# A new written order for the first batch of a fused attention and gated-layer kernel

## The chip, the cores and the metric

The kernel runs on one core of a Trainium2 chip. TensorE multiplies matrices into PSUM, VectorE and ScalarE do element-wise work, and SyncE's queue issues nearly all transfers between the chip's main memory and SBUF. All numbers are 32-bit floats. The metric is the device time of one execution in microseconds (us), and a kernel's time is the median of its runs. The profile is of one execution; its clock starts with the first instruction (the span).

## The reference

For 8 batches of 8 heads, x (512 tokens by 64) and a state (32 rows by 64) look at each other; both results stand under each other, 544 rows a batch, and the heads side by side, 512 columns. A two-layer network with a gate follows.

```python
scores = scale * x @ state.T            # 512 x 32 for each head
xread  = softmax(scores) @ state
scores2 = scale * state @ x.T           # 32 x 512
sread  = softmax(scores2) @ x
y = concat(xread, sread)                # 544 rows a batch, heads side by side: 4352 x 512 (8 batches)
h = y @ w_in                            # d_ff = 2048
g = h * erf(softplus(h))
out = g @ w_out                         # back to 512
```

The kernel doesn't form xread. It multiplies the state of a batch with w_in first ("mixing": m = state times a slice of w_in, for each head) and gets h as the attention weights times m.

## The kernel before, in words

The hidden width 2048 is cut into 4 groups of 512, each group into 4 blocks of 128. Batches 1 to 7 run in a loop of two groups at a time, with seven products in place of eight (L275, L383, L489, L641 and their helpers). Batch 0 is different: no weight is in SBUF yet, so its steps follow the loading of the weights, and nearly everything is interleaved by hand. Its steps are small functions with names, and one string, order0 (L1053 to L1074), lists the names; each is run in that order, and each engine then executes its share in the order written (in_order, L1083). A wait therefore holds up all that stands behind it on the same engine. An engine's own share, not the list as a whole, decides: two neighbours on different engines run side by side.

The names: x0 to x3 turn the tokens (TensorE), st turns the state; s0, s1 are scores, tm0, tm1 turn them, max, less, exp, sum, inv, norm make the softmax over states, ta0, ta1 turn the weights back. An ending _a or _v says whether ScalarE (L756) or VectorE (L757) copies a result from PSUM. m00, m01, m02, m10, m12 and so on mix (group, first block; L908), x and y are halves. h01 is hidden block 1 of group 0 (L919), soft01 its Softplus (L952), erf01 its Erf (L954; erf00+ does two blocks at once, L957), mul01 the product of both (L959, VectorE). p021 is the second-layer product of token block 2, hidden block 1, group 0 (L926): 16 for each group, each of two passes. big, wt (Exp, L854), wz (an inverse), wn, tw and read are the attention in the other direction, u0 and u1 turn the states of the other batches.

i0 to i7 and o0 to o7 are pieces of w_in and w_out, each needing two ScalarE steps (a0 at L166 and a1 at L168) and three VectorE steps (v0 to v2, L171 to L173); i0+ is the second half of piece i0. A `get` issues the load of the next piece (L156) into one of three buffers, in a fixed order of pieces; it waits until the buffer is read. lxq10 to lxq17, lxq2 and lx1 load x of batches 1 and 2 in two layouts, xq1v turns one on VectorE (2.30 us). q, qm, qe, qs, qr, n0, n1, cm and ca are the attention, mixings and sums of batch 1. kept stores w_in in main memory, from where the loop reloads it.

A name with a number, as `4*to1`, first issues so many "warm" products of the identity by itself (warm, L192, through lead) into the bank that the step will use. They compute nothing that is used; each is two passes of 128 columns.

The functions on ScalarE need a table: Exp, Softplus and Erf each have one of their own, and changing from one to another puts an ACT_TABLE_LOAD into the program. So the order of ScalarE's steps decides how many loads there are.

The last 40 names of the list are put in order together with the loop's first instructions. After the list come the first hidden products of batch 1 (L489, with copies at L495 and L504), between them the rest of group 3's p steps, and then the read of batch 1 (L275).

Of the kernel before, what the change touches and what calls it, by code (L numbers as in the profile page):

```python
# [17 lines left out]
def kernel(  # L18
# [78 lines left out]
    def load_xq(b, hs=range(H)):  # L97
# [11 lines left out]
    st = const.tile([P, B, P], F32, name="st")  # L109
    away0 = ring[:, 1, 0].rearrange("p k i t -> p (k i t)")  # L110
    st0 = away0[:, 512:640].rearrange("p (g d) -> p g d", g=2)
    x0 = xin.tile([P, NC, H, D], F32, name="x").rearrange("p c h d -> p (c h d)").rearrange(
        "p (h c d) -> p h c d", h=H, c=NC)
# [931 lines left out]
    for _ in range(3):  # L1045
# [5 lines left out]
    ready = next0()  # L1051

    order0 = """  # L1053
        first x0 x2 x2_v x0_a x3 x3_v st x1 i0a0 st_v s1 i0v0 i0a1 i0v1 x1_a s10_v i0v2 s11_a 2*s0
        tm1 i0+a0 i0+a1 i0+v0 i0+v1 s00_a max1 s01_a tm0 less1 exp1 m00y m001_a i0+v2 max0 i1a0 sum1
        4*to1 m01x m010_a less0 exp0 o0a1 m00x 4*to1 m01y m011_a inv1 norm1 i1a1 4*ta1 u0 o0a0 sum0
        inv0 m000_v norm0 ta0 get ta1_v h001 ta0_a lxq13 o1a1 h01 i1v0 i1v1 soft01 i1v2 lxq16 m02
        m020_a m021_v o0v0 h000 o0v1 soft00 u1 u1_v h02 erf00+ h03 o0v2 mul01 big1 p001 mul00 u0_v
        p011 big0 p010 p030 o1a0 big soft03 lxq17 o1v0 p000 soft02 erf02+ p031 p020 p021 o1v1 o1v2
        wt0 mul03 wt1 p023 wz mul02 wn0 get i2a0 i2v0 get i2a1 i2v1 i3a1 get lxq14 lxq10 p033 p032  # L1060
        tw0 p013 tw0_a p002 i3a0 i2v2 m10 m101_a p022 o2a0 m100_v h10 o2a1 h11 i3v0 i3v1 i3v2 m12
        o2v0 p012 o2v1 m121_v lxq11 get p003 lxq15 lxq12 soft10 m120_v h13 wn1 soft11 o3a0 erf10+
        h12 o3a1 o2v2 mul11 mul10 p110 p100 soft13 p111 p120 get p101 o3v0 o3v1 p131 soft12 o3v2
        erf12+ mul13 p123 p103 i4a0 i4v0 i4a1 mul12 p132 p133 i4v1 i4v2 get i5a1 i5a0 i5v0 i5v1 get
        o4a0 p113 m20 p130 p121 m201_v m200_v h20 i5v2 m22 m220_v m221_v o4a1 o4v0 o4v1 get get p102
        soft20 o5a1 o4v2 p112 o5a0 o5v0 tw1 tw1_v o5v1 erf20 mul20 h21 h23 i6a0 h22 p220 soft21 p210
        o5v2 soft23 erf23 mul23 p230 soft22 erf22 xq1v get i7a1 read read_v p203 mul22 p223 i6a1
        i6v0 i6v1 i6v2 i7a0 p213 p202 q erf21 q1_a qm7 get p222 q0_a p232 qm1 mul21 o6a1 n1 o6a0
        p212 n11_v p231 i7v0 i7v1 n10_a m30 cm0 m300_a m301_a qm0 qm6 p211 p221 get qm8 qe2 qm3 qm5
        qe1 p200 p201 qe3 qm2 qm4 i7v2 n0 n00_a h30 qe0 qs1 qs0 qs2 h31 n01_a m32 p122 soft30 m321_a  # L1070
        m320_a get p233 o6v0 o6v1 o6v2 soft31 erf31 h32 mul31 h33 p311 cm1 qr0 o7a0 qr2 get erf30
        mul30 p331 p301 qr1 cm3 ca0 qr3 p310 soft32 erf32 o7a1 mul32 get ca1 ca2 o7v0 o7v1 lx1 p330
        ca3 p321 soft33 p300 kept erf33 o7v2 lxq2 mul33 cm2 p320
    """  # L1074
    steps0 = order0.split()
    for n, name in enumerate(steps0):
# [246 lines left out]
```

## Time and profile before

| what | value |
|---|---|
| time, median of 3 runs (lowest, highest) | 720.24 us (720.0, 721.69) |
| the profiled execution's own time | 720.67 us |
| its span, first to last instruction | 718.9 us |
| TensorE busy | 710.0 us (99%) |
| VectorE busy | 541.7 us (75%) |
| ScalarE busy | 378.8 us (53%) |
| moved by the transfers | 74.64 MB |
| first second-layer product (L926) | 29.30 us |
| first copy at L495, after the list | 111.95 us |
| read of batch 1 (L275) | 129.99 us |

The profile counts TensorE as busy from a product's start to its modelled end, so short waits between products hide in a busy time of 99%. They show when the starts of rows are set against the number of passes between them. A row names the engine, the source line, the operation, out<-in tiles, the sizes and the count; what stands in brackets is idle time of the engine before it, and what ended it.

### The profile page before, as it was taken

Reading aid. Unit: us, or ns where it says so; the run is one execution under the profiler, and the core shown is the slowest. Engines: PE = TensorE matmul, PEld = TensorE weight load, DVE = VectorE, ACT = ScalarE, POOL = GpSimd, SP = SyncE. Lnnn points to the kernel's source line nnn. Section 1 sums busy time; section 2 is a strip of 40 time slices with the busy share of each in tenths; the row PEclk is TensorE's granted clock in tenths of the full one; section 3 lists DMA queues with packets and bytes.
Section 4 is the critical chain, followed back from the end, with each engine's and each line's share of the span. In section 5 each row is a group of like instructions: output and inputs, shape, how many; then the busy total and the mean of one; then the engine's idle time right before and its main releaser. Section 6 shows DMA issues by size and latency. Waiting matters only on the chain.

```text
span 718.9 us, 10934 instructions
## 1 busy us (share of the span) xinstructions
PE 710.0 (99%) x4275; PEld 560.5 (78%) x4275; DVE 541.7 (75%) x878; ACT 378.8 (53%) x537; POOL 25.2 (4%) x34
## 2 busy tenths in 40 slices
PE   8899999999999999999999999999999999999998
PEld 6344346688878878887888878887888888889997
DVE  5887799889868987788776967697877757664533
ACT  5898986746464625545446436462464535442340
POOL 0000000000100000000000000000000000000000
PEclk9999999999999999999999999999999999999999
DMA  8695597660349163513623280614242321102100
GB/s 268 193 247 200 170 321 178 149 179 30 45 88 220 25 130 51 148 45 89 101 30 146 60 144 5 176 27 131 50 103 84 86 52 26 34 30 30 22 10 29
DMA packets 144067, 74.64 MB, mean 104 GB/s; under 512 B 123024, under 2 KB 132624, under 8 KB 142480
## 3 DMA queue, kind: packets, MB, share of 16 engines
q1 hardware_dynamic: 139152, 65.89, 33.3%
q0 software_dynamic: 4032, 7.34, 7.5%
q8 instruction: 33, 0.54, 0.3%
q10 hardware_dynamic: 832, 0.72, 0.3%
q14 instruction: 18, 0.15, 0.1%
HBM read 49.81 MB, written 20.45 MB: 98 GB/s over the span
## 4 chain that ended last, share of the span: by engine, by line
PE 87%; ACT 7%; DMA 3%; DVE 2%; issue 1%; SPq 0%; ACTq 0%
PE o L641 47%; PE h L489 13%; PE at L489 10%; PE h L534 3%; PE o L616 3%; PE o L926 3%; DMA raw<-in_moe_w_out_dram 2%; PE h L383 2%; PE at L383 2%; ACT L952 1%; PE at L275 1%; ACT raw L168 1%; ACT ring L952 1%; ACT L954 1%; PE h L919 1%
## 5 line engine op out<-in xcount | busy, mean ns | idle before, releaser
L641 PE MATMUL o<-w_out,ring 128*128 128x256 f32 x896 | 203.0, 379 | 0.0
L641 PEld LDWEIGHTS o<-w_out,ring 128*128 128x128 f32 x896 | 169.8, 190 | 24.9 <-DVE ring L1126 0.8
L641 PE MATMUL o<-raw,ring 128*128 128x256 f32 x672 | 161.4, 381 | 0.0
L641 PEld LDWEIGHTS o<-raw,ring 128*128 128x128 f32 x672 | 126.5, 190 | 25.9 <-ACT m L385 9.2
L482 ACT ACTIVATE ring<-ring 128x512 f32<-128x512 f32 x112 | 70.6, 631 | 59.7 <-DVE ring L472 59.1
L489 PE MATMUL h<-aT,m 128*128 128x256 f32 x336 | 81.9, 379 | 0.3 <-ACT ring L495 0.3
L1126 DVE TENSOR_TENSOR ring<-ring 128x1024 f32<-128x1024 f32 (+1 forms) x61 | 70.7, 1201 | 4.5 <-ACT ring L546 4.5
L489 PEld LDWEIGHTS h<-aT,m 128*128 128x128 f32 x336 | 63.8, 190 | 10.6 <-issue 1.2
L472 DVE TENSOR_TENSOR ring<-ring,at 128x512 f32<-128x512 f32 x84 | 57.1, 680 | 16.9 <-PE at L489 15.2
L926 PE MATMUL o<-w_out,ring 128*128 128x512 f32 x128 | 59.9, 602 | 0.1
L626 DVE TENSOR_TENSOR ot<-uv,o 128x256 f32<-128x256 f32 (+1 forms) x56 | 30.9, 552 | 30.1 <-PE o L641 28.1
L472 DVE TENSOR_TENSOR ring<-ring,h 128x512 f32<-128x512 f32 x56 | 38.0, 678 | 20.0 <-PE h L489 19.9
L664 ACT COPY ot<-o 128x256 f32<-128x256 f32 x28 | 10.4, 373 | 77.9 <-PE o L641 77.9
L704 POOL DMA_DIRECT2D out_dram<-ot x28 | 24.5, 946 | 654.9 <-DVE ot L626 556.1
L926 PEld LDWEIGHTS o<-w_out,ring 128*128 128x128 f32 x128 | 23.2, 189 | 28.1 <-issue 22.4
L626 DVE TENSOR_TENSOR ot<-ot,o 128x256 f32<-128x256 f32 x56 | 22.2, 416 | 27.9 <-ACT ot L664 27.7
L504 ACT COPY ring<-h 128x512 f32<-128x512 f32 x28 | 16.4, 587 | 47.9 <-PE h L489 47.9
L673 DVE TENSOR_TENSOR ring<-ring 128x512 f32<-128x512 f32 x56 | 38.6, 689 | 1.4
L674 DVE TENSOR_TENSOR ring<-ring 128x512 f32<-128x512 f32 x56 | 36.2, 684 | 0.0
L385 ACT COPY m<-h 128x512 f32<-128x512 f32 x13 | 7.6, 586 | 46.3 <-PE h L383 46.1
L546 ACT ACTIVATE ring<-ring 128x2048 f32<-128x2048 f32 x16 | 30.5, 1904 | 0.0
L489 PE MATMUL h<-sy,sx 128*128 128x256 f32 x112 | 28.7, 379 | 0.0
(201 smaller groups left out, 963.7 us busy)
## 6 DMA issues: line engine op xcount, KB each, us to landing
w_in<-kept_in SPq DMA_DIRECT2D x7, 2048.0 KB, 8.3
out_dram<-ot SPq DMA_DIRECT2D x33, 256.0 KB, 2.2
raw<-in_moe_w_in_dram SPq DMA_DIRECT2D x16, 512.0 KB, 5.3
raw<-in_moe_w_out_dram SPq DMA_DIRECT2D x8, 1024.0 KB, 5.1
xq<-in_x_dram SPq DMA_DIRECT2D x112, 64.0 KB, 3.2
x<-in_x_dram SPq DMA_DIRECT2D x56, 128.0 KB, 3.1
out_dram<-ot POOLq DMA_DIRECT2D x28, 256.0 KB, 4.5
sc<-xT SPq DMA_DIRECT2D x112, 32.0 KB, 1.9
```

Source lines behind the costliest of these rows:

```text
L383: nc.tensor.matmul(out=ps[k][e][q, :], lhsT=st[r, b, q], rhs=of_group[g][r, :, i, :], start=True, stop=True)
L472: add = lambda o, x, y: nc.vector.tensor_tensor(o, x, y, op=ALU.add)
L482: nc.scalar.activation(out=s[k], in_=hs[k], func=ACTF.Softplus)
L489: nc.tensor.matmul(out=out[:, i], lhsT=x[:, q:q + P], rhs=y, start=(first and i == 0), stop=(i == 1), skip_group_check=not first)
L546: nc.scalar.activation(out=s, in_=s, func=ACTF.Erf)
L626: add = lambda o, x, y: tt(o, x, y, op=ALU.add)
L641: nc.tensor.matmul(out=out, lhsT=lhs[:, i, :], rhs=rhs[:, g, i, :], start=(start and i == 0), stop=(i == GF - 1), skip_group_check=not start)
L673: return [lambda: tt(S1, A21, A22, op=ALU.add), lambda: tt(S2, S1, A11, op=ALU.subtract), lambda: tt(S3, A11, A21, op=ALU.subtract), lambd ...
L674: lambda: tt(S3, A11, A21, op=ALU.subtract), lambda: tt(S4, A12, S2, op=ALU.subtract)]
L704: nc.gpsimd.dma_start(out=rows[2 * h + r][:, c], in_=ot[:, c], accum_op=ALU.add)
L926: nc.tensor.matmul(out=acc[r], lhsT=gT[g][:, i, P * r:P * r + P], rhs=w_out[:, GF * g + i, :], start=(made_of[r] == 1), stop=(made_of[r] = ...
L1126: nc.vector.tensor_tensor(s[:, ks], s[:, ks], hs[:, ks], op=ALU.mult)
```

## The change

The string order0 is written anew, and nothing else. The steps are the same but for some copies that change their engine, and for the warm products: besides the eight of the first step, 14 before (two ahead of s0, four ahead of m01x, m01y and ta1 each), 13 after (three ahead of tm1, six ahead of m01x, four ahead of ta0). The tokens' turns, the two score halves, the pieces' conversions, the p steps, the loads of x of batch 1 (lxq, lx1), the load of xq for batch 2 and kept all change places. The order of the pieces' loads itself stays.

```diff
@@ -1051,26 +1051,26 @@
     ready = next0()
 
     order0 = """
-        first x0 x2 x2_v x0_a x3 x3_v st x1 i0a0 st_v s1 i0v0 i0a1 i0v1 x1_a s10_v i0v2 s11_a 2*s0
-        tm1 i0+a0 i0+a1 i0+v0 i0+v1 s00_a max1 s01_a tm0 less1 exp1 m00y m001_a i0+v2 max0 i1a0 sum1
-        4*to1 m01x m010_a less0 exp0 o0a1 m00x 4*to1 m01y m011_a inv1 norm1 i1a1 4*ta1 u0 o0a0 sum0
-        inv0 m000_v norm0 ta0 get ta1_v h001 ta0_a lxq13 o1a1 h01 i1v0 i1v1 soft01 i1v2 lxq16 m02
-        m020_a m021_v o0v0 h000 o0v1 soft00 u1 u1_v h02 erf00+ h03 o0v2 mul01 big1 p001 mul00 u0_v
-        p011 big0 p010 p030 o1a0 big soft03 lxq17 o1v0 p000 soft02 erf02+ p031 p020 p021 o1v1 o1v2
-        wt0 mul03 wt1 p023 wz mul02 wn0 get i2a0 i2v0 get i2a1 i2v1 i3a1 get lxq14 lxq10 p033 p032
-        tw0 p013 tw0_a p002 i3a0 i2v2 m10 m101_a p022 o2a0 m100_v h10 o2a1 h11 i3v0 i3v1 i3v2 m12
-        o2v0 p012 o2v1 m121_v lxq11 get p003 lxq15 lxq12 soft10 m120_v h13 wn1 soft11 o3a0 erf10+
-        h12 o3a1 o2v2 mul11 mul10 p110 p100 soft13 p111 p120 get p101 o3v0 o3v1 p131 soft12 o3v2
-        erf12+ mul13 p123 p103 i4a0 i4v0 i4a1 mul12 p132 p133 i4v1 i4v2 get i5a1 i5a0 i5v0 i5v1 get
-        o4a0 p113 m20 p130 p121 m201_v m200_v h20 i5v2 m22 m220_v m221_v o4a1 o4v0 o4v1 get get p102
-        soft20 o5a1 o4v2 p112 o5a0 o5v0 tw1 tw1_v o5v1 erf20 mul20 h21 h23 i6a0 h22 p220 soft21 p210
-        o5v2 soft23 erf23 mul23 p230 soft22 erf22 xq1v get i7a1 read read_v p203 mul22 p223 i6a1
-        i6v0 i6v1 i6v2 i7a0 p213 p202 q erf21 q1_a qm7 get p222 q0_a p232 qm1 mul21 o6a1 n1 o6a0
-        p212 n11_v p231 i7v0 i7v1 n10_a m30 cm0 m300_a m301_a qm0 qm6 p211 p221 get qm8 qe2 qm3 qm5
-        qe1 p200 p201 qe3 qm2 qm4 i7v2 n0 n00_a h30 qe0 qs1 qs0 qs2 h31 n01_a m32 p122 soft30 m321_a
-        m320_a get p233 o6v0 o6v1 o6v2 soft31 erf31 h32 mul31 h33 p311 cm1 qr0 o7a0 qr2 get erf30
-        mul30 p331 p301 qr1 cm3 ca0 qr3 p310 soft32 erf32 o7a1 mul32 get ca1 ca2 o7v0 o7v1 lx1 p330
-        ca3 p321 soft33 p300 kept erf33 o7v2 lxq2 mul33 cm2 p320
+        first x0 x0_v x1 x1_a st st_v i0a0 x2 x2_v s0 x3 i0v0 s00_v i0a1 i0v1 i0v2 s01_a tm0 x3_a
+        i0+a0 i0+v0 i0+a1 max0 s1 s10_a i0+v1 s11_a less0 exp0 m00x i1a1 3*tm1 i0+v2 max1 m00y
+        m000_a sum0 m001_a get 6*to1 m01x less1 m01y exp1 lxq14 inv0 norm0 4*ta0 i1a0 sum1 inv1
+        m010_v norm1 u0 o0a0 o0a1 ta1 m011_a ta1_a i1v0 ta0_v h000 i1v1 i1v2 h01 m02 o1a0 o1v0 o0v0
+        h001 o1a1 u1 m021_v m020_v soft01 lxq11 o0v1 o0v2 u0_v get soft00 h03 erf00+ h02 soft02
+        mul00 p020 p000 p010 u1_v soft03 p030 o1v1 mul01 p011 erf02+ big1 p031 p001 p021 big0 big
+        wt1 o1v2 wt0 mul03 mul02 p012 i2a0 wz wn0 tw0 i2a1 p033 i2v0 i2v1 i2v2 get p022 p002 tw0_a
+        i3a0 i3v0 wn1 m10 m101_v i3a1 i3v1 p013 m100_a get o2a0 h11 i3v2 o2a1 h10 get m12 m121_v
+        p023 o2v0 p032 lxq17 p003 soft11 get soft10 erf10+ m120_v h13 h12 o2v1 mul10 o2v2 mul11 o3a0
+        o3a1 p110 i4a0 p120 p101 p130 soft13 lxq10 p121 p111 o3v0 o3v1 i4v0 o3v2 i4a1 i4v1 i4v2
+        lxq13 soft12 erf12+ get get lxq12 p131 p100 mul13 mul12 i5a0 i5v0 i5a1 p123 m20 p113 m200_a
+        p103 m201_a p122 i5v1 get h21 i5v2 m22 h20 o4a0 o4v0 o4a1 o4v1 m220_v o4v2 m221_v tw1 tw1_v
+        soft21 h22 h23 lxq15 o5a0 lxq16 get get o5v0 p133 o5a1 p112 p132 o5v1 o5v2 get soft20 erf20
+        mul20 soft23 p102 p220 soft22 erf22 xq1v mul22 i6a0 i6v0 erf23 mul23 p230 i6a1 read read_a
+        i6v1 i6v2 p210 erf21 mul21 q q1_a qm1 qm3 p203 q0_a qm0 i7a1 qm6 p233 qm2 qm4 n1 n10_a p213
+        n11_a i7a0 i7v0 p201 m30 p221 p223 m301_a i7v1 m300_a o6a1 n0 o6a0 n00_v h31 n01_a h30 get
+        p200 o7a0 get o6v0 p212 soft31 soft30 p211 qm5 i7v2 m32 cm0 cm1 cm3 erf31 p232 erf30 qm7
+        o6v1 kept p222 m321_a m320_a h33 p231 lxq2 mul30 o6v2 p300 qm8 mul31 o7v0 o7a1 o7v1 qe0 qs0
+        qe2 qe3 qe1 qs1 h32 soft32 erf32 p301 get qs2 qr0 qr2 ca0 soft33 get erf33 qr1 qr3 mul32
+        o7v2 p320 ca1 ca3 p311 lx1 p202 p321 cm2 p331 mul33 ca2 p310 p330
     """
     steps0 = order0.split()
     for n, name in enumerate(steps0):
```

## The prediction

> **What bounds the kernel now.** I read the page's totals, then its chain, then the order of time of TensorE and the chain over the first 140 us, because the diff touches only the first batch's list. The page:
>
> ```profile
> PE 710.0 (99%) x4275; PEld 560.5 (78%) x4275; DVE 541.7 (75%) x878; ACT 378.8 (53%) x537; POOL 25.2 (4%) x34
> ...
> PE 87%; ACT 7%; DMA 3%; DVE 2%; issue 1%; SPq 0%; ACTq 0%
> ```
>
> TensorE sets the time, and the new order keeps its products. Only the places where TensorE waits can be won, and all that the list orders lies ahead of the read of batch 1 (L275 at 129.99). From there both programs have the same instructions, so a shift at that mark is the shift of the end. The order of time of TensorE (start, length, operation, passes; a product is two passes):
>
> ```profile
> 29.30 10.03 PE L926 MATMUL o<-w_out,ring 128*128 128x512 f32 x22
> 39.16 0.60 PE L862 MATMUL at<-ident,ring 128*128 128x128 f32 x4
> 39.60 1.88 PE L926 MATMUL o<-w_out,ring 128*128 128x512 f32 x4
> 41.82 0.67 PE L908 MATMUL at<-w_in,ring 64*32 64x256 f32 x16 [0.34 <-DVE w_in L173]
> ...
> 43.38 3.60 PE L919 MATMUL h<-aT,m 128*128 128x512 f32 x8
> 46.91 0.66 PE L908 MATMUL at<-w_in,ring 64*32 64x256 f32 x16
> ...
> 74.52 2.74 PE L926 MATMUL o<-w_out,ring 128*128 128x512 f32 x6
> 78.04 1.10 PE L275 MATMUL at<-x,sc 128*32 128x64 f32 x64 [0.78 <-DVE ring L959]
> 79.07 3.95 PE L926 MATMUL o<-w_out,ring 128*128 128x512 f32 x8
> 82.95 1.09 PE L224 MATMUL at<-xq,st 64*32 64x512 f32 x16
> ...
> 111.26 1.03 PE L489 MATMUL h<-sy,sx 128*128 128x256 f32 x4
> 112.57 1.13 PE L489 MATMUL h<-aT,m 128*128 128x256 f32 x4 [0.28 <-ACT ring L495]
> ...
> 129.99 1.10 PE L275 MATMUL at<-x,sc 128*32 128x64 f32 x64
> ```
>
> A 512-wide pass costs 0.429 (eight of L919 take 3.43 in the chain), a 256-wide one 0.216. What a row takes to the next row's start beyond its passes is wait. From 43.38 to 46.91 it is 3.53 for 8 x 0.429 = 3.43: 0.10 goes with the change to a block of small products, and that recurs at each such block whatever the order. The rest:
>
> - 29.30 to 39.16: 9.86 - 22 x 0.429 = 0.42
> - 39.60 to 41.82: 2.22 - 1.72 - 0.10 = 0.40, the mixing m10, which waits for weight piece i2
> - 74.52 to 78.04: 3.52 - 2.57 - 0.10 = 0.85, the read of batch 0, which waits for a score bank that mul23 frees
> - 79.07 to 82.95: 3.88 - 3.43 - 0.20 = 0.25
> - 111.26 to 112.57: 1.31 - 0.86 = 0.45, and 0.11 after it: the first products after the list wait for L495's copy, which stands behind the last Erf on ScalarE
>
> Together 2.5 us. That is all the list can give after 29.30. Before 29.30, TensorE has little to do and waits for others; what counts is when the first second-layer product (L926) starts. The chain there, start and length:
>
> ```profile
> 16.20 6.04 DMA raw<-in_moe_w_out_dram
> ...
> 22.32 1.16 ACT raw L168
> ...
> 23.50 1.28 ACT L952
> ...
> 24.79 0.60 ACT ring L952
> 25.39 0.26 ACT m L756
> 25.65 0.50 ACT ring L952
> ...
> 26.17 1.28 ACT L957
> ...
> 27.47 1.06 ACT ring L957
> 28.52 1.04 ACT w_out L166
> ```
>
> The second w_out piece (o1) lands at 22.24; ScalarE, idle for 1.9, converts its low words, loads the Softplus table, makes two Softplus with a copy between, loads Erf, makes Erf; VectorE multiplies (0.69), and L926 starts: 22.24 to 29.30 is 7.06.
>
> **What the Trainium skill says.** "ScalarE: Activation LUTs", What ACT_TABLE_LOAD costs: about 1283 ns for a load, whatever the set, and some 1380 of drain. The trace agrees with the first (1.28 in every row) and shows no such drain (the next activation starts 0.02 later); I use 1.28. "TensorE: Matmul & The Clock Gate", What's actually happening: the clock is halved by default, is released after about 3.4 us of activity and falls back after an idle window of that length. The trace agrees on the start (the first 16 passes take 3.75, 0.234 each; a later row of eight takes 1.16) and shows 1.00 from then on; no run here shows a fall-back.
>
> **The change part by part.**
>
> *First w_out product (cost 0.8).* Up to the load of o1 the load queue issues the same transfers in the same order, so the landing at 22.24 stands. Before, only o1a1 (1.16) stands between landing and the Softplus table load; o1a0 comes after the first Erf, the row at 28.52. Now o1a0 and o1a1 both stand ahead of soft01: plus 1.05 (1.14 less the 0.09 by which neighbours on ScalarE overlap). The copy m020 (0.26) goes to VectorE, which waits for ScalarE here and hides it. 7.06 + 1.05 - 0.26 = 7.85, so L926 starts at 30.1. Bounds: were the load so early that ScalarE isn't waiting at 20.5, both lists would start alike (0); I see nothing beyond 1.05. I take 0.8.
>
> *m10 (wait 0.6 in place of 0.4).* From the end of the first Erf (28.52) to the end of i2's last conversion step (41.78) the chain is ScalarE (o1a0, two tables with Softplus and Erf, the Exp table and the two wt steps, i2a0, i2a1), then VectorE's L172 and L173: 13.26. Without o1a0 it is 12.2, and the Erf ends 0.8 later, so i2 is ready at about 41.55. TensorE now has 12 products ahead of m10 instead of 13 (p013 moved behind it): 30.1 + 24 x 0.429 + 0.45 for the turn tw0 + 0.10 = 40.95. It waits 0.6.
>
> *Group 2 on ScalarE (gains 0.85 + 0.25).* Before, group 2 goes soft20, erf20, soft21 and soft23, erf23, soft22, erf22: six table loads, and from 67.70 to 84.77 ScalarE has no pause. Now soft21 and soft20, erf20, soft23 and soft22, erf22, erf23: four. That takes 2 x 1.28 = 2.57 us from the stretch of ScalarE that makes TensorE wait at 78.04, three times the wait; no wait is left there. The long VectorE turn xq1v (2.30) still stands ahead of mul22, but the read needs only the free bank.
>
> *End of the list (gains 0.56).* In the chain ScalarE works from 94.04 to 111.95 without a pause. Two table loads less, two copies more (0.25 and 0.38: read and one m copy come from VectorE) leave it 1.9 ahead; the copy at L495 was 0.45 late, so TensorE doesn't wait. This holds though everything starts 0.8 later, since TensorE is later by the same.
>
> *The 0.42 at 29.30 to 39.16 (gains 0.3 to 0.4).* VectorE's order has the inverse wz ahead of mul02. wz waits 1.6 for the Exp steps (the waits list it as z L212 behind ring L854), starts at 37.20, and mul02 ends only at 38.15; the products of hidden block 2 (p033 runs, p032 waits) come up short of it. Now mul03 and mul02 stand ahead of wz and follow the second Erf, which ended at 34.33: even 0.8 later they are done by 36.5, while the first product of hidden block 2, p012, comes ninth, at 30.1 + 8 x 0.858 = 37.0.
>
> *Warm products.* Before 2 + 4 + 4 + 4 = 14, after 3 + 6 + 4 = 13, each two passes of 0.112. The six ahead of m01x cost 1.34 and lie in TensorE's wait for the bank copies m000 and m001, which stand on ScalarE behind an Exp and a 1.16 conversion; they cost nothing while that wait, some 2.8, is longer. Without it: 1.3.
>
> *Loads.* The second half's transfers stay the same; x of batch 1 (8 issues, landed 95.41) moves behind the three stores of kept_in and the 16 xq issues. Those ended at 111.65, so x lands by about 115, 14 before L275 needs it; the reload of w_in stays behind them as it was, near 112. On SP's queue all that waits behind the third store is these 24 issues: no cost.
>
> Sum: 0.8 + 0.6 - 2.5 = -1.1; with 0.1 of the first bullet kept for the restart after a wait, -1.0. The profiled execution took 720.67 (span 718.9, 1.8 around it), 0.4 above the median of three; taken from the median 720.24, it gives **719.2**, with the mark L275 near 129.0.
>
> **Rivals.**
>
> *All of it pays (0.14).* If o1 lands by 20.5 to 21, as other loads of that size do (4.7 to 5.2 after issue, not 6.04), the 0.8 shrinks to near 0 and the m10 wait goes too: 720.24 - 2.5 = 717.7, faster. Against it: o1 queues behind the eight small state loads, which finish at 17.62.
>
> *The waits only move (0.09).* The new order leaves little room at m10, the bank of the batch-1 scores and L495's copy; three such waits of 0.4 eat the gain: 720.4, up to 721.
>
> *Slower: the clock (0.09).* Before, warm products stand at 8.97 and 12.79; now none come between 4.5 and the three at tm1, near 11 (where the turns of the scores stand before: 10.62 and 11.68), and what TensorE does there is turns and small score products. If an idle window passes and the clock halves, each microsecond of dense product costs one more. Up to 20 there is little dense work and others set the pace; the price comes if the half clock reaches the L919 products after it, 3.4 us of them in one window: 719.2 + 3.4 = 722.6. It decides from 3.2 us of dense work on. For it: the gap is longer than now. Against: the six ahead of m01x follow, and a similar gap did nothing here.
>
> *As forecast (0.68).* Own range 718.2 to 720.6.
>
> **How the numbers follow.** 0.3% (2.2 us) is about what a measurement of this kernel tells from no change, so the limits are 718.1 and 722.4. Faster is the first rival, 0.14. Same is the forecast and most of the second, 0.75. Slower is the clock and a rest of mishaps, 0.11. For 8 in 10 the range goes from 717.5, the first rival with both waits gone, to 721.0, the second's end; the clock case stays outside.
>
> **What would show it.** Right: L926 first at about 30.1, with two 128x1024 conversions between o1's landing and the first Softplus table load; a wait ahead of m10 near 41.6; no wait at the first read and none at L495; 21 table loads up to the first copy at L495, for 23; L275 of batch 1 near 129.0. Wrong: a clock below 1.00 after 5 us; L926 before 29.5; a wait over 0.3 between 60 and 113; x of batch 1 landing after 125.

## The result, and the profile after

The changed kernel took 719.15 us (median of 18 runs, 718.45 to 720.73) where the kernel before took 721.08 on the same chip (18 runs, 719.75 to 723.02): a ratio of 0.9976, 95% interval [0.9968, 0.9983]. That is 1.7 us of 720, inside the 0.3% within which the prediction counts a result as no change; the time that it named was 719.2. The profiled execution took 718.98, its span 717.2 where before's was 718.9.

The page of the changed kernel, the totals and the shares of the chain:

```profile
PE 707.9 (99%) x4273; PEld 560.0 (78%) x4273; DVE 541.1 (75%) x876; ACT 377.3 (53%) x537; POOL 25.2 (4%) x34
...
PE 94%; DMA 3%; ACT 2%; DVE 0%; issue 0%; SPq 0%
```

ScalarE held 7% of the chain and now holds 2%; TensorE's part went from 87% to 94%. The order of time of TensorE after the change (start, length, operation, passes, idle time ahead):

```profile
29.37 7.99 PE L926 MATMUL o<-w_out,ring 128*128 128x512 f32 x18 [0.81 <-DVE ring L959]
37.19 0.63 PE L862 MATMUL at<-ident,ring 128*128 128x128 f32 x4
37.66 2.74 PE L926 MATMUL o<-w_out,ring 128*128 128x512 f32 x6
40.84 0.67 PE L908 MATMUL at<-w_in,ring 64*32 64x256 f32 x16 [0.44 <-DVE w_in L173]
...
71.82 5.31 PE L926 MATMUL o<-w_out,ring 128*128 128x512 f32 x12
77.06 1.10 PE L275 MATMUL at<-x,sc 128*32 128x64 f32 x64
78.10 1.12 PE L926 MATMUL o<-w_out,ring 128*128 128x512 f32 x2
79.15 1.09 PE L224 MATMUL at<-xq,st 64*32 64x512 f32 x16
...
109.18 1.03 PE L489 MATMUL h<-aT,m 128*128 128x256 f32 x4
110.04 1.03 PE L489 MATMUL h<-sy,sx 128*128 128x256 f32 x4
110.91 1.10 PE L489 MATMUL h<-aT,m 128*128 128x256 f32 x4
...
128.31 1.10 PE L275 MATMUL at<-x,sc 128*32 128x64 f32 x64
```

With the prediction's prices (0.429 for a 512-wide pass, 0.216 for a 256-wide one, 0.10 for a change to small blocks):

- 29.37 to 37.19 is 7.82 for 18 x 0.429 = 7.72: the 0.42 us of waits are gone.
- 37.66 to 40.84 is 3.18 for 2.57 + 0.10: m10 waits 0.51 (0.40 before).
- 71.82 to 77.06 is 5.24 for 12 x 0.429 = 5.15, and 0.10 for the small blocks: the read waits for nothing (0.85 before).
- 109.18 to 110.91 is 1.73 = 8 x 0.216: no wait for L495's copy (0.45 + 0.11 before).

From the first L926 to the read of batch 1 it is 98.94 us where it was 100.69, and the first L926 stands at 29.37 where it stood at 29.30. So of the 1.68 us at the mark L275, the stretch behind 29.3 gives 1.75 and the start takes 0.07.

The chain of the changed kernel ahead of the first L926 (start, length, what):

```profile
16.27 5.31 DMA raw<-in_moe_w_out_dram
21.58 0.02 issue
21.61 1.14 ACT w_out L166
22.75 1.07 ACT raw L168
23.82 0.02 issue
23.84 1.28 ACT L952
25.13 0.01 issue
25.14 1.08 ACT ring L952 x2
...
27.53 1.06 ACT ring L957
```

The two conversions (L166, L168) stand between the landing and the Softplus table load, as the prediction said. But the load landed 5.31 us after its issue and not 6.04, and that took back nearly all that the second conversion costs.

### The profile page after: what moved, and what is told of

Read it like the earlier page. It is cut to its first block, busy times and chain, and to the rows that moved or that the text cites. A ratio compares the mean times of both kernels' runs of the same rounds, so it can differ in the third digit from the quotient of the medians.

```text
span 717.2 us, 10922 instructions
## 1 busy us (share of the span) xinstructions
PE 707.9 (99%) x4273; PEld 560.0 (78%) x4273; DVE 541.1 (75%) x876; ACT 377.3 (53%) x537; POOL 25.2 (4%) x34
## 4 chain that ended last, share of the span: by engine, by line
PE 94%; DMA 3%; ACT 2%; DVE 0%; issue 0%; SPq 0%
PE o L641 48%; PE h L489 13%; PE at L489 10%; PE o L926 6%; PE h L534 3%; PE o L616 3%; DMA raw<-in_moe_w_out_dram 2%; PE h L383 2%; PE at L383 2%; PE h L919 1%; PE at L919 1%; PE at L275 1%; PE o L224 1%; DMA x<-in_x_dram 1%; PE at L908 1%; ACT L957 0%
## 5 line engine op out<-in xcount | busy, mean ns | idle before, releaser
L489 PE MATMUL h<-aT,m 128*128 128x256 f32 x336 | 81.9, 379 | 0.0
L489 PEld LDWEIGHTS h<-aT,m 128*128 128x128 f32 x336 | 63.8, 190 | 10.1 <-issue 1.4
L926 PE MATMUL o<-w_out,ring 128*128 128x512 f32 x128 | 59.5, 599 | 0.8 <-DVE ring L959 0.8
L926 PEld LDWEIGHTS o<-w_out,ring 128*128 128x128 f32 x128 | 23.5, 190 | 28.3 <-issue 25.3
L504 ACT COPY ring<-h 128x512 f32<-128x512 f32 x28 | 16.4, 586 | 47.9 <-PE h L489 47.9
L495 ACT COPY ring<-h 128x512 f32<-128x512 f32 x28 | 16.4, 586 | 24.6 <-PE h L489 24.6
```

Of the source, the lines that this page charges most:

```text
L489: nc.tensor.matmul(out=out[:, i], lhsT=x[:, q:q + P], rhs=y, start=(first and i == 0), stop=(i == 1), skip_group_check=not first)
L926: nc.tensor.matmul(out=acc[r], lhsT=gT[g][:, i, P * r:P * r + P], rhs=w_out[:, GF * g + i, :], start=(made_of[r] == 1), stop=(made_of[r] = ...
```

## The experiments

My theory was the prediction's sum: the list gains where it takes TensorE's waits away, each wait counted by itself, and loses at the start. Its rivals were that waits only move, and that the clock decides. Every kernel here computes the same result; only warm products, whose results nobody uses, are added or left out. Times are ratios to the kernel before, run beside them; the new list stands at 0.9976 on that scale, and 0.001 is 0.7 us.

### The order of group 2's activations put back (in the new list)

```diff
-  soft21 h22 h23 ... soft20 erf20 mul20 soft23 p102 p220 soft22 erf22 xq1v mul22 i6a0 i6v0 erf23 mul23 p230
+  h22 h23 ... soft20 erf20 mul20 soft21 p102 p220 soft23 erf23 mul23 soft22 erf22 xq1v mul22 i6a0 i6v0 p230
```

> The new list, with group 2's activations put back into the order of six table loads: soft20, erf20, soft21, erf23 behind soft23, soft22, erf22. My theory (the shorter ScalarE stretch of group 2 took away the waits between 74 and 83 us): two table loads more, 2.57 us of ScalarE, of which at least the 1.1 us of removed waits come back there; 720.2 to 721.3 on a scale where the new list is 719.15. Rival (the waits there went for another reason, as the place of xq1v): no wait over 0.2 us near 75 to 83, time within 0.4 us of the new list.

Measured: 721.51 us, 1.0014 [1.0008, 1.0021]. That is 0.0038 or 2.7 us above the new list, and slower than the old one. TensorE's order of time in this run:

```profile
76.69 1.10 PE L275 MATMUL at<-x,sc 128*32 128x64 f32 x64
77.72 1.12 PE L926 MATMUL o<-w_out,ring 128*128 128x512 f32 x2
79.28 1.04 PE L224 MATMUL at<-xq,st 64*32 64x512 f32 x2 [0.43 <-DVE ring L959]
80.76 1.43 PE L224 MATMUL at<-xq,st 64*32 64x512 f32 x14 [0.44 <-ACT sn L281]
```

and ScalarE's:

```profile
74.67 1.28 ACT L952 ACT_TABLE_LOAD   x1
75.97 0.60 ACT L952 ACTIVATE ring<-at 128x512 f32<-128x512 f32 x1
76.58 1.28 ACT L954 ACT_TABLE_LOAD   x1
77.88 0.63 ACT L954 ACTIVATE ring<-ring 128x512 f32<-128x512 f32 x1
...
80.47 0.24 ACT L281 COPY sn<-at 128x128 f32<-128x128 f32 x1
```

The read itself isn't late (L926 to read 47.71 us, 47.69 in the new list). The loss is right behind it: from the read to the next block L1016 it is 7.35 us (76.69 to 84.04) where the new list takes 5.02 (77.06 to 82.08). The two table loads come back, 2 x 1.28 = 2.56, and the copy of the read (L281), which the new list puts on ScalarE, comes at 80.47 where it came at 78.23; the second half of L224 waits for it. So within the new list group 2's order is worth the table loads nearly whole, 2.3 us in the profile. The prediction had priced it at 1.1, the waits that it removed from the old list, where VectorE copies the read and does not stand behind these loads.

### The same order given to the old list, alone

```diff
-  erf20 mul20 ... soft21 p210 o5v2 soft23 erf23 mul23 p230 soft22 erf22 xq1v
+  erf20 mul20 ... soft21 soft23 p210 o5v2 soft22 erf23 mul23 p230 erf22 xq1v
```

> Edit to the kernel before, alone: soft23 ahead of p210 and soft22 ahead of erf23, so that group 2's activations go soft, erf, soft, soft, soft, erf, erf as in the new list and take four table loads where they took six. Same computation. By the prediction's sum two loads of 1.28 us off ScalarE in a stretch where it is the last releaser are worth some of the 1.1 us that the waits at 78 to 83 us cost: 719.5 to 720.0, 0.9985 to 0.9992 of before, and no wait at the first read. By the rival, that what pays is where the new list puts the copies of h and o around these activations, not the number of loads: no gain (0.9995 to 1.001), the wait at the read stays or moves by less than 0.3 us.

Measured: 720.67 us, 1.0002 [0.9994, 1.001]: no gain, though the profile counts 21 table loads up to the first L495 copy, as in the new list, and 23 in the old. That is the rival's time, but the wait moved by more than the 0.3 that it allowed. The read's row:

```profile
79.06 1.10 PE L275 MATMUL at<-x,sc 128*32 128x64 f32 x64 [1.51 <-DVE ring L959]
```

The wait grew from 0.78 to 1.51. The chain goes through ScalarE: with soft22 in front, erf23 begins at 77.66 in place of 76.63 (0.29 of this is the later start of the whole profile, 0.49 is soft22), so mul23 frees the score bank later. What the two loads then save behind the read (51.53 us from read to read, 51.95 before) is lost ahead of it. Table loads saved are no gain by themselves: here they were saved behind the step that TensorE waits for, and the Softplus that was moved went ahead of it.

### Half of one list, half of the other

> A list of two halves: the new list up to its step tw1_v (just ahead of soft21, about 68 us in), and from there every step that is left in the old list's order. Same computation. Working from the waits in the two profiles: the new first half brings 0.1 to 0.3 us (0.42 us of waits at 29 to 39 us gone, m10's wait 0.1 us longer), and the old second half brings back the waits at the first read, at 79 to 83 us and at the first L489 products, 0.88 + 0.25 + 0.56 us. Expected 720.3 to 720.7 where before is 720.6 (0.9996 to 1.0001). If the first half is where the gain was made, 719.2 or less (0.998).

> The other way round: the old list up to its step p102 (just ahead of soft20, about 69 us in), and from there every step that is left in the new list's order. Same computation. The waits of the second half (0.88 + 0.25 + 0.56 = 1.7 us) should be gone and those at 29 to 42 us be as before: 718.9 to 719.3 (0.9977 to 0.9982). If the new second half pays only behind the new first half, because loads, copies and activations stand elsewhere where it begins, there is a wait of over 0.5 us at the first read again and the time is 719.9 or more (0.999 or more).

The lists themselves are those that the diff shows, joined at the named steps:

```diff
# new, then old
   ... h20 o4a0 o4v0 o4a1 o4v1 m220_v o4v2 m221_v tw1 tw1_v
-  soft21 h22 h23 lxq15 o5a0 lxq16 get get o5v0 p133 ...
+  lxq16 lxq15 p132 p133 get p102 soft20 o5a1 p112 o5a0 o5v0 ...
# old, then new
   ... h20 i5v2 m22 m220_v m221_v o4a1 o4v0 o4v1 get get p102
-  soft20 o5a1 o4v2 p112 o5a0 o5v0 tw1 tw1_v o5v1 ...
+  p122 h21 o4v2 tw1 tw1_v soft21 h22 h23 o5a0 get o5v0 ...
```

Measured: new-then-old 722.07 us, 1.0016 [1.0009, 1.0023]; old-then-new 724.15 us, 1.0044 [1.003, 1.0057]. Both are slower than either whole list; I had expected 0.9996 to 1.0001, and 0.9977 to 0.9982. If the effects of the halves (+0.0016 and +0.0044) could be added, the whole change would cost 0.6%; it gains 0.24%.

New-then-old shows the old waits back (0.90 ahead of the read, 0.94 ahead of L489 where the old list had 0.28), and one stretch of half clock early, of which more below. In old-then-new the two rows with waits are

```profile
76.33 1.99 PE L926 MATMUL o<-w_out,ring 128*128 128x512 f32 x4 [1.18 <-DVE ring L959]
80.67 1.66 PE L275 MATMUL at<-x,sc 128*32 128x64 f32 x64 [2.35 <-DVE ring L959]
```

and their cause is in its list of waits (engine, line, waited for: us in total, times, longest):

```profile
ACT ring L952 <- PE h L919: 6.4, 1, 6.4
```

ScalarE has the Softplus table loaded by 64 us and then stands 6.4 us, since the new half asks for soft21 first, and its h21 stands here behind h20, the mixing m22 and two products, p102 and p122. TensorE makes h20 from 64.32 on and h21 only from 68.55 on; in the new list h21 comes first, at 63.73. So soft21 starts at 70.46 here and at 65.64 in the new list, and ScalarE's row of table loads ends as much later. This settles the second expectation for its rival: the new second half pays only behind a first half that makes the hidden products of group 2 in its order. It says so for this one joint; others weren't tried.

### Two edits at m10

The inverse wz behind mul02, in the old list:

```diff
-  wt0 mul03 wt1 p023 wz mul02 wn0
+  wt0 mul03 wt1 p023 mul02 wz wn0
```

> Edit to the kernel before: wz behind mul02 in place of ahead of it, the order of these two in the new list. Same computation. The wait of 0.33 us for mul02 (of the 0.42 us at 29 to 39 us in the profile of before) should go. By the prediction's rival that m10 absorbs it, m10's wait grows from 0.44 to about 0.75 us and the time stays: 720.6 (0.9997 to 1.0003). If it is worth its face value: 720.3 (0.9995).

Measured: 720.35 us, 0.9995 [0.9988, 1.0002]. TensorE's order of time:

```profile
39.62 1.88 PE L926 MATMUL o<-w_out,ring 128*128 128x512 f32 x4
42.16 0.67 PE L908 MATMUL at<-w_in,ring 64*32 64x256 f32 x16 [0.65 <-DVE w_in L173]
```

From the first L926 to L862 it is 29.64 to 39.19, 9.55 for 9.44 of passes: 0.31 of the 0.42 is gone. m10's wait went from 0.34 to 0.65, by the same 0.31. The profile follows the rival's arithmetic: m10 takes up what the earlier place gives. The times can't tell 0 from 0.3 us.

The second output-weight chunk's conversion o1a0 moved ahead of o1a1 in the old list, as in the new one:

```diff
-  ... ta0_a lxq13 o1a1 h01 ...   p011 big0 p010 p030 o1a0 big
+  ... ta0_a lxq13 o1a0 o1a1 h01 ...   p011 big0 p010 p030 big
```

> The list before, with one step moved: o1a0 ahead of o1a1, so that both conversions of the o1 piece stand between its landing and the first Softplus, as in the new list. Prediction's step: the first second-layer product starts 0.8 to 1.05 us later. What that is worth at the end: by the prediction's sum the wait at m10 changes only because a product moved, so the end is 0.8 to 1.05 later (722.0 where before is 721.1). Rival: ScalarE's chain up to piece i2 is the same length in either order, so m10 stands where it stood, its wait of 0.4 is used up, and the end is 0.4 to 0.6 later or less.

Measured: 720.99 us, 1.0009 [1.0001, 1.0017], some 0.6 us more, as the rival had it. But this is not the 1.05 us of the conversion less m10's wait. The profile is of one of the longer executions (722.52), and in it the edit does more:

```profile
27.24 5.40 PE L919 MATMUL at<-aT,m 128*128 128x512 f32 x8 [2.29 <-ACT m L756]
```

The copy m020 (L756), which stays on ScalarE in this list, now stands behind both conversions. TensorE waits 2.29 us for it and then makes these eight passes, 3.43 us of work, in 5.23, mostly at half clock. L926 starts 9.69 behind the landing, 2.63 later than in the old list. From there to the read of batch 1 it wins 1.31 back, since 0.42 behind 29 us, m10's 0.40 and 0.48 of the wait at the read are gone. Seven of the 21 executions have a mean clock of 0.998 or less, and their median is 722.5; the other 14 have 720.7, where the old list has 720.6. So most of the 0.6 us goes with the clock; where it holds, the conversion ahead costs too little to be told.

### o1 behind the first Softplus, in the new list, and a product ahead of m10

```diff
# first run
-  m02 o1a0 o1v0 o0v0 h001 o1a1 u1 m021_v m020_v soft01 lxq11 ... p030 o1v1
+  m02 o0v0 h001 u1 m021_v m020_v soft01 o1a0 o1a1 lxq11 ... p030 o1v0 o1v1
# second run: besides
-  i3a0 i3v0 wn1 m10 m101_v i3a1 i3v1 p013
+  i3a0 i3v0 wn1 p013 m10 m101_v i3a1 i3v1
```

> The new list with both conversions of the o1 piece (o1a0, o1a1) behind the first Softplus soft01, o1v0 ahead of o1v1. ScalarE then doesn't wait for the landing of o1 (1.75 us in the new list's profile) before it loads the Softplus table. My theory, that the first second-layer product is paced by ScalarE's steps behind that landing: L926 starts about 1 us earlier, near 28.3, and since i2 follows on the same engine, m10 moves too: 717.9 to 718.4 where the new list is 719.15. Rival (the landing isn't what paces it, TensorE's own hidden products h000 and h01 are): L926 near 29.4 and the same time.

> Edit to the changed kernel: o1a0 and o1a1 (ScalarE's preparation of the second output-weight chunk) moved from ahead of soft01 to behind it, o1v0 to just ahead of o1v1, and the product p013 moved ahead of m10. Same computation. By my theory two waits are left in the new list between 14 and 42 us: ScalarE's 1.7 us for that load, and TensorE's 0.5 us ahead of m10's mixings; the first move alone (run f2) gained nothing since m10's wait took it. With a product (0.86 us) put in front of m10 that wait closes, and 0.4 to 0.6 us come off: about 718.3 where the new list is 718.9 on this chip (0.9968 of before). The rival, that the stretch is paced by ScalarE's and VectorE's own chain of activations and casts and the product only moves from one side of m10 to the other: 718.8 +- 0.3, a 0.44 us longer wait somewhere behind m10.

Measured: 718.73 us, 0.9975 [0.9968, 0.9983], and 718.75 us, 0.9975 [0.9965, 0.9986]: neither can be told from the new list. In the first, ScalarE no longer waits for the load, but it waits 1.33 us for the hidden product h01 (L919) instead; L926 starts at 29.61 and not near 28.3, and m10 waits 0.47 (0.44 in the new list). That is the rival of the first expectation. The clock fell early in this profile, though, and the second edit's, where it held, has L926 at 28.72; how much of the start is the clock's stays open, and the times gain nothing either way. In the second, m10 doesn't wait, and the wait stands one step further:

```profile
40.54 0.66 PE L908 MATMUL at<-w_in,ring 64*32 64x256 f32 x16
41.67 3.70 PE L919 MATMUL h<-aT,m 128*128 128x512 f32 x8 [0.46 <-ACT m L756]
```

The product p013 was what TensorE did while ScalarE copied the mixings out of their bank (0.38 us at 41.24). Moved ahead of m10, it covers the conversion of i2 and no longer covers the copy. That is the rival's picture, and the forecast of 0.4 to 0.6 us falls.

### A load made late, in both lists

> Edit to the kernel before: the transfers of one eighth of the next batch's x (lxq11, 2 issues on SP a piece) put in two times more just ahead of the fifth get, so that the output-weight chunk which it loads is issued about 2.6 us later (at about 44.5 us). The same data is loaded again to the same place: the computation is the same. If slack for late loads is what the old list lacks, the load's consumers come late and TensorE waits: +1.3 to +2.0 us (1.0018 to 1.0028). If the old list has slack here too: under +0.3 us (1.000 to 1.0004).

> Edit to the changed kernel: lxq17's transfers put in four times more just ahead of the fifth get, so that the output-weight chunk which it loads is issued about 4.2 us later (at about 45 us in place of 40.9). The same data is loaded again to the same place: the computation is the same. If the new list has the slack for late loads that its description claims: no more than +0.4 us over the new list, 0.9976 to 0.9982 of before. If it is no slacker than the old one, delay less a couple of us comes through: +1.3 us or more, 0.9994 or above.

```diff
# old list
-  o2v1 m121_v lxq11 get p003
+  o2v1 m121_v lxq11 lxq11 lxq11 get p003
# new list
-  o2a1 h10 get m12
+  o2a1 h10 lxq17 lxq17 lxq17 lxq17 get m12
```

Repeated transfers to one place wait for each other (SyncE's queue stands 3.1 and 7.9 us for them in the two profiles), so both gets came 4.5 us later, which makes the two comparable: 41.83 to 46.29 in the old list, 40.87 to 45.38 in the new one. Measured: old 726.23 us, 1.0076 [1.0064, 1.0089]; new 723.01 us, 1.0032 [1.0021, 1.0043], 0.0056 or 4.0 us above the new list. The old list's 5.5 us miss the 1.3 to 2.0 that I had expected of a delay of 2.6; the new list's answer is the one given for no more slack. The long wait in the old list's run, and in the new list's:

```profile
56.70 11.38 PE L926 MATMUL o<-w_out,ring 128*128 128x512 f32 x22 [2.82 <-DVE ring L959]
```

```profile
62.92 2.07 PE L926 MATMUL o<-w_out,ring 128*128 128x512 f32 x2 [2.98 <-DVE ring L959]
```

The new list does have more slack for that one load: it lands at 45.73 and is converted at 48.91, behind the Erf, where the old list's landed at 47.02 and was converted at 47.51. But the w_in pieces that follow it on the queue land at 51.08 and are converted at 51.10; in the run they are late by the same 4 us. ScalarE waits 1.92 for the load itself and 1.84 for them, where in the old list it waits 3.14 for the load. The slack moved from one load to the next, and the delay costs TensorE 2.8 us in one list and 3.0 in the other. Most of the rest of the 4 to 5.5 us is the clock. Stretches of the old list's run, then of the new list's (stretch, its length, TensorE's busy time, granted clock, DMA share, GB/s):

```profile
55.54:58.95 3.41, 2.25 (x4) 0.82 0.98 343
58.95:62.36 3.41, 3.41 (x7) 0.68 0.45 110
62.36:65.77 3.41, 3.41 (x9) 1.00 0.49 202
```

```profile
58.95:62.36 3.41, 0.99 (x3) 1.00 0.89 300
62.36:65.77 3.41, 2.85 (x18) 0.55 1.09 320
65.77:69.18 3.41, 3.41 (x16) 0.95 0.89 186
```

Within about 1 us of the end of each wait the clock falls to half, for 3.41 us in all: 0.82 and 0.68 are 0.18 and 0.32 short of full, together half of one such stretch, and so are 0.55 and 0.95. Dense products lose half of that, 1.7 us: the row of 22 passes takes 11.38 where it took 9.61. In the new list 0.25 (later start) + 2.98 + 1.7 = 4.9, against a shift of 133.28 - 128.31 = 4.97 at L275. By the medians the new list loses 1.5 us less than the old one, at the edge of what the intervals tell; the profiles, shifted by 4.97 and 5.10, don't show it, and the new list's is of its slowest execution.

### The warm products

None (the 13 left out), and six more ahead of m01x, both in the new list:

```diff
# none: tm1, to1 and ta0 without 3*, 6* and 4*
# twelve
-  m001_a get 6*to1 m01x
+  m001_a get 12*to1 m01x
```

> The new list without its 13 warm products (those of the first step stay). My theory: they lie in waits and the clock doesn't need them: within 0.3 us of the new list's 719.15, clock 1.00 in all stretches. Rival (they keep the clock up, and the new places of them are worth something): the granted clock falls below 1.00 somewhere between 7 and 25 us, products there take up to twice as long, 1 to 4 us slower.

> Edit to the changed kernel: twelve warm products (12*to1) ahead of m01x where it has six; none of their results is used, the computation is the same. TensorE's six take 1.60 us in a wait that lasted 0.35 us longer, up to ScalarE's copy for the mixings, so six more (about 1.6 us at full clock) overrun it by about 1.2 us. By the prediction's step that warm products cost nothing while covered, that overrun is on the path only as far as TensorE sets the pace there: the first 128x512 output product (29.4 us in the new list) 0.5 to 1.2 us later, and 719.2 to 719.8 (0.998 to 0.999 of before) since the rest passes it on unshortened. If VectorE and the weight load set the pace up to 29 us: no change, 718.7 to 719.0.

Measured: none 719.36 us, 0.9984 [0.9978, 0.9991]; twelve 719.43 us, 0.9988 [0.998, 0.9996]. Both are some 0.6 to 0.9 us above the new list, at the edge of what the intervals tell. Without them, in the profile, TensorE runs at half clock for three stretches on end, from 11.81 to 22.05 us:

```profile
11.21:14.62 3.41, 2.11 (x20) 0.59 1.07 387
14.62:18.03 3.41, 1.93 (x20) 0.50 0.64 98
18.03:21.44 3.41, 2.99 (x10) 0.50 0.94 308
```

All 21 executions without them have a mean clock of 0.992 to 0.997, those of the new list 0.997 to 1.0. So the warm products shorten the half clock; they don't prevent it, as four profiles with them show one such stretch too. Ten microseconds of half clock cost some 0.6 in the median, and the profile shows none of it behind the load: the first L926 follows the load's landing by 7.78 in this run and by 7.79 in the new list. Whether the clock has a part in the later landing isn't shown. With twelve, the time came out in the range I gave (719.2 to 719.8), but its profile doesn't show the reason I gave: the products overrun (14.44 to 17.73, no wait behind them), yet L926 at 29.74 is again the landing (21.93) plus 7.81.

## Why the prediction was right

**The waits behind 29.3: right, place by place.** For m10 a wait of 0.6 was forecast and 0.51 found. The 0.3 to 0.4 at 29 to 39 us is gone, as said, and so are the waits at the read, behind it and at L495; 21 table loads stand where 23 stood. Without the first step the sum was 0.6 - 2.5 + 0.1 = -1.8; the profile has -1.75. x of batch 1 was issued by 108.2 and landed by about 111, far from deciding. The six warm products ahead of m01x stayed inside their wait, which was 1.96 (12.99 to 14.95) and not some 2.8.

**The first L926: the step that failed.** "Up to the load of o1 the load queue issues the same transfers in the same order, so the landing at 22.24 stands", with 0.8 to pay. The path did get longer: landing to L926 is 7.05 to 7.09 in five profiles with the old start and 7.78 to 7.83 in six with the new one (two runs that move o1, and the edit of the old start, aside). The term of 0.8 was right in size, 0.74. What didn't stand is the landing, which the prediction carried over from one profile because nothing changes ahead of the load. In the profiles with the old start it came 5.2 to 6.0 us after its issue (mean of six 5.74), in those with the new start 4.9 to 5.4 (mean of eight 5.22), and the issue was earlier too: landing at 22.53 and 21.70 in the mean. So the first L926 stands at 29.54 in the mean of the five and 29.57 in that of the six: nothing lost, as far as starts that spread from 28.9 to 30.3 can tell. Why the load is faster wasn't tried and stays open; the new list issues four transfers of x right behind it where the old one issues six.

**Its rival "all of it pays"** named just this, a load that takes 4.7 to 5.2, and gave it 0.14, wanting m10's wait to go as well. The load came 0.66 earlier, which is what it took; m10's wait stayed. At 719.15 and a ratio of 0.9976, the median lies at the forecast of 719.2, but the shift of 1.7 in the profile and in the ratio lies between the forecast's 1.0 and this rival's 2.5. That the time agrees to 0.1 is luck: the forecast was 0.7 to 0.9 short of the shift, and the kernel before took 721.08 beside the new one, 0.84 more than the 720.24 that the prediction started from. The two errors cancel.

**"The waits only move"** is right at m10 (the edits of wz and of p013 each gave their wait to a neighbour) and wrong for the rest.

**The clock.** Its mechanism is real and its price was too high. The profile after shows 1.00 throughout, but five of the eight profiles with the new start and its edits fell to half somewhere from 11.2 us on, for one stretch or, without warm products, three; none of the six with the old start did so early. From 7.6 to 11.0 us TensorE is busy for 1.6 to 2.6 us in the new start and 3.1 to 3.4 in the old, as that rival had read from the gap between the warm products; the six ahead of m01x, named against it, come too late (12.99 in the profile after; the falls began from 11.2 to 12.3).

How often the new list itself falls can be read from the mean clock of each execution. One stretch at half takes 0.5 x 3.41 / 718 = 0.0024 from it, and the profiles fit: 0.999 or 1.0 for those without a stretch, 0.997 or 0.998 for one, 0.995 for two, 0.993 for three. By this count 8 of the new list's 18 executions fell, and 3 of 147 of the old list, run beside the experiments. The medians of the 8 and of the other 10 are 719.3 and 719.0, too close to be told apart. So the clock turned against the new list in nearly every second execution and took some 0.3 us or nothing there, not 3.4. The prediction asked for 3.2 us of dense work under the half clock, and the work there is light: turns, small products and warm ones.

The Trainium skill ("TensorE: Matmul & The Clock Gate", What's actually happening) puts a fall after an idle window of about 3.4 us. The length of a stretch at half agrees with that window (3.41), but here no single wait was that long (1.51 to 1.83): a TensorE that was only partly idle in the 3.4 us before fell too.

**Did the change do what it says?** Slack for long ScalarE steps: yes, that is the gain. Slack for late loads: not shown; the one run leaves room for some 1.5 us of it, at the edge of what its interval tells.

## What to carry to other kernels

In an order written out by hand, count the gain of a moved step only together with the steps that feed it: the same saving of two table loads was worth 2.3 us in the list built for it and nothing in the other, and at the one joint tried, either half of the new list was worse than none of it. Before closing a small wait ahead of one step, ask what the filler was covering behind it; two edits at m10 only moved waits of 0.3 to 0.5 us. Where a stall left TensorE idle for 2 to 3 us ahead of dense products, it cost its length and then up to 1.7 us of half clock. And read the clock of every execution, not only of the profiled one: an edit can cost nothing in most of them and 2 us in a third.

## What the runs showed that I had not expected

The clock falls after less idle time than I took. Idle times of 2.29 (o1a0 moved), 2.35 (old list, then new), 2.82 and 2.98 us (late loads) were each followed by a stretch of 3.41 us at half clock, which began 0.2 us before to 1.0 us after the next products did; idle times of up to 1.5 us ahead of dense products were not. In the early part, where the work is light, less sufficed, and the eight profiles with the new start and its edits part cleanly by one wait, that of the block L815 near 10 us: 1.51, 1.53, 1.66, 1.83 and 1.83 us in the five whose clock fell, 0.78, 1.42 and 1.44 in the three where it didn't. TensorE's busy time from 7.61 to 11.02 parts them as well (1.58 to 1.90 us in the five, 1.92 to 2.58 in the three), so which of the two counts stays open; no run varied either by itself. The new list's own profile is one of the three, by 0.07 us, which fits 8 of its 18 executions having fallen. In the profile of the changed kernel:

```profile
9.64 0.65 PE L815 MATMUL at<-ident,ring 128*128 128x128 f32 x4 [1.44 <-DVE ring L757]
```

Warm products ahead of that block, where the new list has none, weren't tried.
